# Batch 0's attention scores straight from strided q in two 64x64 tiles; w_in's first parts in four buffers; batch 1's first k and q behind batch 0's last v

## The chip, the cores and the metric

The kernel runs on one core of a Trainium2 chip. The metric is the time of one execution in device microseconds, the median of several runs. A NeuronCore has five engines that each work through their own instructions in order: TensorE (PE; its weight loads are shown as PEld), VectorE (DVE), ScalarE (ACT), GpSimd (POOL) and SyncE (SP), which here only issues DMA transfers. They wait for each other through semaphores.

## The reference, cut to what matters

Four batches (B = 4) of 576 tokens. A windowed attention over 8 heads of 64 feeds a second attention with 4 experts, of which two are chosen per token, and that feeds a mixing stage with sine and cosine and a last matrix product. Only the first two stages are touched.

```python
def _attn_ref(q, k, v):
    scores = scale * np.matmul(q, k.transpose(0, 1, 3, 2))
    rel = pos[:, None] - pos[None, :]
    mask = (rel >= 0) & (rel < 64)
    scores = np.where(mask, scores, -1000000000.0)
    attn = softmax(scores)
    return np.matmul(attn, v)

def _moe_ref(x, w_gate, wq, wk, wv, wo):
    logits = x @ w_gate
    for e in range(E):
        q, k, v = x @ wq[e], x @ wk[e], x @ wv[e]
        a = softmax(causal(scale * q @ k.T))
        out += chosen(e) * (a @ v @ wo[e])
```

(`softmax`, `causal` and `chosen` stand for the lines of the reference that spell them out.)

## The kernel before, in words

**The first attention** (`phase_a`, L236 to 316). The 8 heads are taken as 4 pairs (`hp`), one head in partitions 0 to 63 and one in 64 to 127. A pair's q lies as [128, 64, 9]: for each feature, 64 positions within a block by 9 blocks, so the 64 positions of one block stand 9 floats (36 bytes) apart. A pair is worked in three units (`g`) of three blocks of 64 queries; a batch has 12 units. I number batch 0's units 0 to 11. One unit is:

- q is copied into a tile `QD` [128, 3, 128] that is block diagonal: head 0's 64 columns in the upper half of the partitions, head 1's in the lower, zeros elsewhere, cleared once at the start (L167 to 170). In batch 0 DVE copies the upper half (L260) and ACT the lower (L258); in the later batches POOL copies both (`pool_mul`, L82, called from L256).
- three score products of 128x128 weights (`QD`) by 128 columns of k (L263), into a PSUM bank `as`;
- DVE adds the band mask and takes the row maximum (L268), ACT takes exponentials with row sums (L276), DVE sums and inverts (L281, L282), POOL multiplies (L283);
- PE transposes (L288, tile `apt`), DVE copies out (L291, `apv`; from batch 1 on ACT, L293), PE multiplies by v in 64-column tiles (L145 and L148, through `together`, tile `ao`), and the result is split into a high part (ACT, L87, `x0h`) and a low part (DVE, L90, `x0l`).

**The second attention** needs `w_in`, split into a high part `wih` (cast by ACT, L202) and a low part `wil` (POOL, L207; DVE for part of it, L209). `load_w` (L191) brings the four row blocks of its first 516 columns through two staging buffers (pool tag `bms`), then the rest. `vg_gates` (L346) makes values and gates from x (tile `vg`, 60 gate products a batch), `qk` (L319) makes queries and keys (tile `qk`), and `attn` (L403) does the attention; there POOL scales by the gates (L453, tiles `bms` and `bpd`).

**What sets the order.** The Python code yields after pieces of work, and `merge` (L45) interleaves several such generators by costs written by hand; the tile framework then schedules each engine's instructions from its own model of time. So a changed line can move instructions far behind it. The first `merge` (L651) runs batch 0's `phase_a` beside `load_w` for w_in's first columns; the second (L657) runs `qk(0, 0)`, `vg_gates(0)`, half of batch 1's `phase_a` and the rest of w_in. All loads of q, k, v and w_in after the first stand on SP's queue in one order. `fetch` (L219) loads a pair's q and k; `tc.issue_after(x)` keeps an instruction behind x in the schedule. v has four buffers, q and k two each.

## Time and profile before

| | |
|---|---|
| median of 3 runs | 528.53 us (528.49 to 529.69) |
| profiled execution | 528.16 us, of which span 526.4 us |
| busy: PE | 506.6 us (96%), 4372 instructions |
| busy: ACT | 329.6 us (63%) |
| busy: DVE | 323.1 us (61%) |
| busy: POOL | 304.6 us (58%) |
| read from HBM | 31.28 MB |

The profile is of one execution. Its span runs from the first to the last instruction. An fp32 product leaves two records on PE, so three products are shown as x6. A line number can be that of a helper: L93 to L95 are one three-part product, L145 and L148 the products issued through `together`, L82 is `pool_mul`.

### The profile page before, as it was taken

The numbers are of one execution on the slowest core, as the hardware profiler recorded it, in microseconds if no ns is written. First come the engines' busy times: TensorE is split into PE (matmuls) and PEld (weight loads), VectorE is DVE, ScalarE is ACT, GpSimd is POOL, SyncE is SP. The second block draws the span as 40 slices with busy tenths as digits, with TensorE's granted clock in tenths as the row PEclk, the third lists the DMA queues.
The fourth block names the chain that finished last, engine by engine and source line by source line (L and its number), as shares of the span: only waits on it lengthen the run. The fifth ranks groups of instructions, "written<-read, shape, count | busy, mean of one in ns | idle before, by whom it ended". The sixth has DMA issues, their size and how long they took to land.

```text
span 526.4 us, 12343 instructions
## 1 busy us (share of the span) xinstructions
PE 506.6 (96%) x4372; PEld 475.5 (90%) x4372; DVE 323.1 (61%) x1244; ACT 329.6 (63%) x1045; POOL 304.6 (58%) x464
## 2 busy tenths in 40 slices
PE   8879999999999999999998999999999999999997
PEld 6669888899998998989787998999999999999997
DVE  5876887858778597558988787553325324533312
ACT  7977698866878768677788977551437136523410
POOL 5798789664848842247876676951475226531420
PEclk9999999999999999999999999999999999999999
DMA  7865224222314421112004121002000200011002
GB/s 248 253 185 169 97 60 147 64 67 92 103 34 134 142 76 32 32 29 73 37 2 159 62 82 42 1 0 80 12 2 1 68 24 1 1 57 35 1 1 91
DMA packets 21086, 36.80 MB, mean 70 GB/s; under 512 B 2336, under 2 KB 13600, under 8 KB 21024
## 3 DMA queue, kind: packets, MB, share of 16 engines
q1 hardware_dynamic: 19008, 31.22, 18.7%
q10 hardware_dynamic: 2016, 4.79, 2.7%
q8 instruction: 35, 0.57, 0.5%
q14 instruction: 27, 0.22, 0.2%
HBM read 31.28 MB, written 4.72 MB: 68 GB/s over the span
## 4 chain that ended last, share of the span: by engine, by line
PE 70%; DVE 11%; ACT 6%; POOL 6%; issue 3%; DMA 3%; ACTq 0%; POOLq 0%; DVEq 0%
PE y L95 6%; PE y L93 6%; PE y L94 6%; PE as L263 3%; PE c L95 3%; PE c L94 3%; PE c L93 3%; PE th L93 3%; PE th L95 3%; PE th L94 3%; PE bpt L464 2%; PE qk L93 2%; PE qk L95 2%; PE qk L94 2%; PE apt L288 2%
## 5 line engine op out<-in xcount | busy, mean ns | idle before, releaser
L90 POOL TENSOR_TENSOR z<-zf,z 128x256 fp32r<-128x256 f32 x72 | 52.9, 749 | 87.3 <-ACT z L87 86.9
L93 PE MATMUL y<-wkh,z 128*128 128x288 f32 x288 | 86.4, 301 | 0.5 <-DVE x2T L595 0.5
L94 PE MATMUL y<-wkl,z 128*128 128x288 f32 x288 | 85.3, 296 | 0.0
L95 PE MATMUL y<-wkh,z 128*128 128x288 f32 x288 | 84.7, 297 | 0.0
L276 ACT ACTIVATE ams<-ams,anm 128x128 f32<-128x128 f32 x144 | 56.6, 396 | 4.5 <-DVE anm L268 4.1
L93 PEld LDWEIGHTS y<-wkh,z 128*128 128x128 f32 x288 | 54.2, 188 | 1.4 <-DVE x2T L595 0.6
L94 PEld LDWEIGHTS y<-wkl,z 128*128 128x128 f32 x288 | 54.2, 188 | 0.0
L95 PEld LDWEIGHTS y<-wkh,z 128*128 128x128 f32 x288 | 53.9, 188 | 0.0
L283 POOL TENSOR_TENSOR ams<-ams,arc 128x384 f32<-128x384 f32 x48 | 40.8, 850 | 18.5 <-DVE arc L282 7.7
L87 ACT CAST z<-zf 128x256 fp32r<-128x256 f32 x72 | 27.6, 404 | 37.6 <-DVE zf L562 15.7
L441 ACT ACTIVATE bms<-bms,bnm 64x64 f32<-64x64 f32 (+4 forms) x80 | 45.0, 563 | 8.5 <-DVE bnm L436 7.9
L82 POOL TENSOR_SCALAR QD<-qt 64x192 f32<-64x192 f32 x72 | 39.6, 551 | 16.0 <-PE as L263 10.1
L562 DVE TENSOR_TENSOR zf<-xk,ang 128x256 f32<-128x256 f32 x64 | 25.4, 420 | 36.4 <-ACT ang L549 19.4
L547 ACT ACTIVATE ang<-ang 128x256 f32<-128x256 f32 x36 | 14.6, 416 | 51.9 <-DVE ang L546 51.8
L263 PE MATMUL as<-kt,QD 128*128 128x128 f32 x288 | 43.5, 288 | 3.1 <-ACT x0h L87 1.3
L263 PEld LDWEIGHTS as<-kt,QD 128*128 128x128 f32 x288 | 37.5, 197 | 6.8 <-ACT x0h L87 1.5
L268 DVE CUSTOM_DVE_ANT_0 ams<-as,cst 128x128 f32<-128x128 f32 x144 | 34.7, 283 | 6.3 <-PE as L263 3.1
L93 PE MATMUL th<-wth,cx 128*128 128x256 f32 x128 | 36.5, 285 | 2.1 <-DVE bnm L436 1.5
L436 DVE CUSTOM_DVE_ANT_0 bms<-bs,mb 64x64 f32<-64x64 f32 (+4 forms) x80 | 32.5, 423 | 9.3 <-PE bs L434 4.9
L94 PE MATMUL th<-wtl,cx 128*128 128x256 f32 x128 | 36.0, 281 | 0.0
L608 DVE SCALAR_TENSOR_TENSOR x2T<-c,x2T 128x288 f32<-128x288 f32 x32 | 14.5, 457 | 34.2 <-PE c L95 34.0
L95 PE MATMUL th<-wth,cx 128*128 128x256 f32 x128 | 35.4, 283 | 0.0
(198 smaller groups left out, 1742.3 us busy)
## 6 DMA issues: line engine op xcount, KB each, us to landing
vt<-in_dram SPq DMA_DIRECT2D x48, 192.0 KB, 3.1
kt<-in_dram SPq DMA_DIRECT2D x15, 320.0 KB, 3.0
qt<-in_dram SPq DMA_DIRECT2D x16, 288.0 KB, 3.2
out_dram<-x2T SPq DMA_DIRECT2D x32, 144.0 KB, 1.8
w64k<-in_dram SPq DMA_DIRECT2D x5, 576.0 KB, 3.7
w64k<-in_dram ACTq DMA_DIRECT2D x4, 576.0 KB, 3.7
w64t<-in_dram SPq DMA_DIRECT2D x4, 512.0 KB, 3.8
w64c<-in_dram ACTq DMA_DIRECT2D x8, 256.0 KB, 2.8
```

Source lines behind the costliest of these rows:

```text
L82: nc.gpsimd.tensor_scalar(out=out, in0=in_, scalar1=by, scalar2=1.0, op0=ALU.mult, op1=ALU.mult)
L87: nc.scalar.copy(out=dst_h, in_=src)
L90: eng_l.tensor_sub(out=dst_l, in0=src, in1=f32(dst_h))
L93: nc.tensor.matmul(out, wh, xh, start=first, stop=False)
L94: nc.tensor.matmul(out, wh, xl, start=False, stop=False)
L95: nc.tensor.matmul(out, wl, xh, start=False, stop=last)
L263: nc.tensor.matmul(s[:, i, :], QD[g][:, i], kt[:, 64 * blk : 64 * blk + 128], start=True, stop=True)
L268: nc.vector.tensor_tensor_reduce(out=ms[:, i, :], in0=s[:, i, :], in1=ma0 if (g == 0 and i == 0) else ma1, scale=-0.125, scalar=3.0e38, op ...
L276: nc.scalar.activation(out=ms[:, i, :], in_=ms[:, i, :], func=AF.Exp, bias=nm[:, i : i + 1], scale=-1.0, accum_out=sm[:, i, 0:1],)
L283: nc.gpsimd.tensor_mul(out=ms, in0=ms, in1=rc.unsqueeze(2).to_broadcast([P, 3, P]))
L436: nc.vector.tensor_tensor_reduce(out=ms[:m, a:z], in0=s[:m, : z - a], in1=mb[:m, mo + a : mo + z], scale=-0.125, scalar=nm[:m, 0:1] if ci ...
L441: ex = nc.scalar.activation(out=ms[:m, :w], in_=ms[:m, :w], func=AF.Exp, bias=nm[:m, ci : ci + 1], scale=-1.0, accum_out=ss[:m, i, 0:1])
```

## The change

Four things are changed.

1. In batch 0 a unit's scores no longer go through `QD`. For each of the three blocks, two products of 64x64 weights are issued, one per head: the weights are q itself, read from its load tile at the stride of 9 floats, and the 64 rows of one head in k are the moving part. Head 0 uses partitions 0 to 63 of its operands and of the result, head 1 64 to 127. The six products go through `together`, so they stand behind each other in the schedule. The clearing of `QD` moves behind that of `KL`.
2. The four row blocks of w_in's first 516 columns are staged in four buffers, two of tag `bms` and two of tag `zc` (which w_o's staging uses later), instead of two.
3. `paced` replaces `delay`: the costs that `merge` counts for `load_w` are 0.75, 0.1, 0.1, 0.1, 0.35 instead of 0.9 and then 0.1 each, with the same total.
4. Batch 1's and later loads of k and q are scheduled behind the last load of v of batch 0.

```diff
--- before.py
+++ after.py
@@ -165,9 +165,6 @@
 
 
     QD = [ap.tile([P, 3, P], F32, name=f"QD{i}") for i in range(3)]
-    for i in range(3):
-        nc.vector.memset(QD[i][0:64, :, 64:128], 0.0)
-        nc.gpsimd.memset(QD[i][64:128, :, 0:64], 0.0)
 
     AS = [ap.tile([P, 3, 2], F32, name=f"AS{i}") for i in range(4)]
     BS = [bp.tile([P, 2, 2], F32, name=f"BS{i}") for i in range(4)]
@@ -187,12 +184,15 @@
     for e in range(E):
         z = slice(64 - 64 * (e % 2), 128 - 64 * (e % 2))
         nc.gpsimd.memset(f32(KL[e][z]), 0.0)
+    for i in range(3):
+        nc.vector.memset(QD[i][0:64, :, 64:128], 0.0)
+        nc.gpsimd.memset(QD[i][64:128, :, 0:64], 0.0)
 
     def load_w(src, n, dst_h, dst_l, tag):
-        pool, bufs = (bp, 2) if tag == "bms" else (cp, 2)
         for c in range(n):
             h, l = dst_h(c), dst_l(c)
-            st = pool.tile([P, h.shape[1]], F32, tag=tag, bufs=bufs, name=f"wst{c}")
+            pool, home = (cp, "zc") if tag == "zc" or tag == "both" and c >= 2 else (bp, "bms")
+            st = pool.tile([P, h.shape[1]], F32, tag=home, bufs=2, name=f"wst{c}")
             with tc.issue_after(last_load[0].ins):
                 nc.sync.dma_start(st, src[c * P : (c + 1) * P])
             w = h.shape[1]
@@ -210,6 +210,7 @@
             yield 0.1
 
     last_load = [None]
+    last_v = [None]
     late = [None]
     gated = [None]
     X = {b: xbuf[b % 2] for b in range(B)}
@@ -229,8 +230,9 @@
             nc.sync.dma_start(qt, qT[b, hp])
             last_load[0] = nc.sync.dma_start(kt, kT[b, hp])
         else:
-            last_load[0] = nc.sync.dma_start(kt, kT[b, hp])
-            nc.sync.dma_start(qt, qT[b, hp])
+            with tc.issue_after(last_v[0].ins):
+                last_load[0] = nc.sync.dma_start(kt, kT[b, hp])
+                nc.sync.dma_start(qt, qT[b, hp])
         return qt, kt
 
     def phase_a(b, hps):
@@ -243,25 +245,31 @@
             for g in range(3):
                 n = f"{b}{hp}{g}"
                 vt = ap.tile([P, 3, 2, D], F32, tag="vt", bufs=4, name=f"vt{n}")
-                nc.sync.dma_start(vt, vw[b, hp, :, 3 * g : 3 * g + 3])
+                v = nc.sync.dma_start(vt, vw[b, hp, :, 3 * g : 3 * g + 3])
+                if b == 0:
+                    last_v[0] = v
                 if b == 0 and hp == 0 and g == 2:
                     nc.sync.dma_start(cst[:, 3 * P :], consts[:, 3 * P :])
                 if b == 0 and 0 < hp < NP - 1 and g == 0:
                     ahead[0, hp + 1] = fetch(0, hp + 1)
                 s = bank([P, 3, P], "bs" if b == 0 and (g + hp) % 3 else "as", f"as{n}")
-                for h in range(2):
-                    r = slice(64 * h, 64 * h + 64)
-                    src = qt[r, :, 3 * g : 3 * g + 3].rearrange("p d n -> p n d")
-                    if b > 0:
-                        pool_mul(QD[g][r, :, r], src, 1.0)
-                    elif h:
-                        nc.scalar.copy(out=QD[g][r, :, r], in_=src)
-                    else:
-                        nc.vector.tensor_copy(out=QD[g][r, :, r], in_=src)
-                for i in range(3):
-                    blk = 3 * g + i
-                    nc.tensor.matmul(s[:, i, :], QD[g][:, i],
-                                     kt[:, 64 * blk : 64 * blk + 128], start=True, stop=True)
+                src = qt[:, :, 3 * g : 3 * g + 3].rearrange("p d n -> p n d")
+                if b == 0:
+
+                    for f in together():
+                        for i in range(3):
+                            blk = 3 * g + i
+                            for h in range(2):
+                                r = slice(64 * h, 64 * h + 64)
+                                f(s[r, i, :], qt[r, :, blk], kt[r, 64 * blk : 64 * blk + 128], start=True, stop=True)
+                else:
+                    for h in range(2):
+                        r = slice(64 * h, 64 * h + 64)
+                        pool_mul(QD[g][r, :, r], src[r], 1.0)
+                    for i in range(3):
+                        blk = 3 * g + i
+                        nc.tensor.matmul(s[:, i, :], QD[g][:, i],
+                                         kt[:, 64 * blk : 64 * blk + 128], start=True, stop=True)
                 ms = ap.tile([P, 3, P], F32, tag="ms", bufs=4, name=f"ams{n}")
                 nm = ap.tile([P, 3], F32, tag="nm", bufs=4, name=f"anm{n}")
                 for i in range(3):
@@ -644,12 +652,18 @@
         yield cost
         yield from gen
 
+    def paced(costs, gen):
+        yield costs[0]
+        for cost in costs[1:]:
+            next(gen)
+            yield cost
+
 
     warm = bank([P, KN['WM']], "g", "warm")
     for _ in range(WARM):
         nc.tensor.matmul(warm, mb[:, :P], mb[:, : KN['WM']], start=True, stop=True)
     merge((20, phase_a(0, (0, 1, 2, 3))),
-          (KN["CW"][4], delay(0.9, load_w(w_in[:, :W0], NC, lambda c: wih[:, c, :W0], lambda c: wil[:, c, :W0], "bms"))))
+          (KN["CW"][4], paced((0.75, 0.1, 0.1, 0.1, 0.35), load_w(w_in[:, :W0], NC, lambda c: wih[:, c, :W0], lambda c: wil[:, c, :W0], "both"))))
     pool_mul(mb[:, S - P :], cst[:, 3 * P : 4 * P], 1.0)
     for i in range(2):
         nc.gpsimd.memset(VD[i][0:64, :, 1], 0.0)
```

The new order on three engines, word for word; in the names, digits are batch, pair and unit (`ams011` is batch 0, pair 1, unit 1 of the pair) and what follows the underscore is a buffer's number. Line numbers of the change are by its own file, so L284 there is L276 of the kernel before, L271 is L263, L291 is L283 and L461 is L453.

ACT from its first computing instruction on, before:

```order
L258 ACT_TABLE_LOAD
L258 COPY QD0_95<-qt00_135 64x3x64
L258 COPY QD1_96<-qt00_135 64x3x64
L258 COPY QD2_97<-qt00_135 64x3x64
L258 COPY QD0_95<-qt01_141 64x3x64
L276 ACTIVATE ams000_153,AS1_105<-ams000_153,anm000_154 128x128 x3
L258 COPY QD1_96<-qt01_141 64x3x64
L276 ACTIVATE ams001_188,AS2_106<-ams001_188,anm001_189 128x128 x3
L258 COPY QD2_97<-qt01_141 64x3x64
L276 ACTIVATE ams002_224,AS3_107<-ams002_224,anm002_225 128x128 x2
L258 COPY QD0_95<-qt02_253 64x3x64
L276 ACTIVATE ams002_224,AS3_107<-ams002_224,anm002_225 128x128
```

and with the change:

```order
L284 ACT_TABLE_LOAD
L284 ACTIVATE ams000_154,AS1_99<-ams000_154,anm000_155 128x128 x3
L284 ACTIVATE ams001_190,AS2_100<-ams001_190,anm001_191 128x128 x3
L284 ACTIVATE ams002_227,AS3_101<-ams002_227,anm002_228 128x128 x3
L284 ACTIVATE ams010_267,AS0_98<-ams010_267,anm010_268 128x128 x3
L284 ACTIVATE ams011_303,AS1_99<-ams011_303,anm011_304 128x128 x3
L284 ACTIVATE ams012_339,AS2_100<-ams012_339,anm012_340 128x128 x3
L87 CAST x0h_88<-ao000_172 128x192
L202 CAST wih_73<-wst0_406 128x516
L202 CAST wih_73<-wst1_446 128x516
L284 ACTIVATE ams020_379,AS3_101<-ams020_379,anm020_380 128x128 x2
L202 CAST wih_73<-wst2_486 128x516
```

The copies of q are gone, the exponentials of the first six units follow each other, and the four casts of w_in (three of them shown) come behind them.

PE around `qk000`, the first q/k projection of batch 0 (`as110` is a score unit of batch 1), before:

```order
L93 MATMUL vg00_617<-wih_73,x0h_88 128x260
L94 MATMUL vg00_617<-wil_74,x0h_88 128x260
L263 MATMUL as110_850<-kt11_845,QD0_95 128x128 x3
L95 MATMUL vg00_617<-wih_73,x0l_89 128x260
L93 MATMUL vg02_776<-wih_73,x0h_88 128x260
L94 MATMUL vg02_776<-wil_74,x0h_88 128x260
L145 MATMUL ao032_581<-apv032_579,vt032_555 64x64
L148 MATMUL ao032_581<-apv032_579,vt032_555 64x64 x5
L93 MATMUL qk000_599<-x0h_88,wih_73 128x288
L94 MATMUL qk000_599<-x0l_89,wih_73 128x288
```

and with the change, from the same place on:

```order
L93 MATMUL vg00_629<-wih_73,x0h_88 128x260
L94 MATMUL vg00_629<-wil_74,x0h_88 128x260
L145 MATMUL ao032_593<-apv032_591,vt032_566 64x64
L148 MATMUL ao032_593<-apv032_591,vt032_566 64x64 x5
L95 MATMUL vg00_629<-wih_73,x0l_89 128x260
L93 MATMUL vg02_788<-wih_73,x0h_88 128x260
L94 MATMUL vg02_788<-wil_74,x0h_88 128x260
L93 MATMUL qk000_611<-x0h_88,wih_73 128x288
```

and, seven rows further on, from the ninth of that projection's twelve products on:

```order
L95 MATMUL qk000_611<-x0h_88,wil_74 128x288
L93 MATMUL qk000_611<-x0h_88,wih_73 128x288
L94 MATMUL qk000_611<-x0l_89,wih_73 128x288
L95 MATMUL qk000_611<-x0h_88,wil_74 128x288
L271 MATMUL as100_649<-kt10_644,QD0_95 128x128 x3
L95 MATMUL vg02_788<-wih_73,x0l_89 128x260
```

Before, `as100`, `as101`, `as102` and `as110` stand ahead of `qk000`; now the first of them, `as100`, follows that projection's twelve products. Ahead of `qk000` stand all 12 units of batch 0 and 32 gate products in both.

POOL in the second half of batch 0's first attention (`QD` from `qt10` is batch 1's q, `wil` from 128x516 the low part of w_in's first columns), before:

```order
L207 TENSOR_TENSOR wil_74<-wst0_469,wih_73 128x516
L283 TENSOR_TENSOR ams011_298<-ams011_298,arc011_306 128x384
L207 TENSOR_TENSOR wil_74<-wst1_473,wih_73 128x516
L283 TENSOR_TENSOR ams012_333<-ams012_333,arc012_341 128x384
L82 TENSOR_SCALAR QD0_95<-qt10_631 64x3x64 x2
L283 TENSOR_TENSOR ams020_372<-ams020_372,arc020_380 128x384
L82 TENSOR_SCALAR QD1_96<-qt10_631 64x3x64 x2
L207 TENSOR_TENSOR wil_74<-wst2_512,wih_73 128x516
L283 TENSOR_TENSOR ams021_407<-ams021_407,arc021_415 128x384
L82 TENSOR_SCALAR QD2_97<-qt10_631 64x3x64 x2
L283 TENSOR_TENSOR ams022_442<-ams022_442,arc022_450 128x384
L207 TENSOR_TENSOR wil_74<-wst3_551,wih_73 128x516
```

and with the change:

```order
L207 TENSOR_TENSOR wil_74<-wst0_406,wih_73 128x516
L207 TENSOR_TENSOR wil_74<-wst1_446,wih_73 128x516
L207 TENSOR_TENSOR wil_74<-wst2_486,wih_73 128x516
L291 TENSOR_TENSOR ams020_379<-ams020_379,arc020_387 128x384
L207 TENSOR_TENSOR wil_74<-wst3_526,wih_73 128x516
L291 TENSOR_TENSOR ams021_419<-ams021_419,arc021_427 128x384
L291 TENSOR_TENSOR ams022_459<-ams022_459,arc022_467 128x384
L291 TENSOR_TENSOR ams030_499<-ams030_499,arc030_507 128x384
L291 TENSOR_TENSOR ams031_539<-ams031_539,arc031_547 128x384
L291 TENSOR_TENSOR ams032_575<-ams032_575,arc032_583 128x384
L82 TENSOR_SCALAR QD0_95<-qt10_643 64x3x64 x2
L82 TENSOR_SCALAR QD1_96<-qt10_643 64x3x64 x2
```

The splits of w_in stand closer together, and the q tiles of batch 1 come only behind batch 0's last product (`ams032`).

On SP's queue the four loads of w_in's first columns now follow pair 3's q and k, ahead of v of unit 4; before, the third and fourth stood behind v of units 6 and 7, and batch 1's first q ahead of v of unit 4. Batch 1's first k and q now follow the last v of batch 0.

## Rows read from the trace of the kernel before

**Rows 1.** Windows; stretch, then busy us (records) of each engine, PEclk, DMA share, GB/s.

```profile
4.74:41.05 36.31, 30.43 (x308) 25.74 (x309) 27.49 (x164) 30.63 (x122) 27.31 (x43) 1.00 0.77 239
...
28.00:44.00 16.00, 13.34 (x142) 11.71 (x141) 12.02 (x62) 12.22 (x52) 15.20 (x23) 1.00 0.64 193
44.00:60.00 16.00, 16.00 (x159) 15.61 (x158) 11.33 (x63) 12.43 (x49) 10.49 (x22) 1.00 0.23 67
...
35.88:64.53 28.65, 28.38 (x283) 27.15 (x282) 21.24 (x106) 19.90 (x77) 22.29 (x45) 1.00 0.41 123
```

**Rows 2.** Chain of waits, in order of time: start us, us, what.

```profile
39.60 0.67 PE as L263 x6
40.27 0.12 PE vg L95
...
40.62 0.20 PE ao L145
...
41.12 0.33 PE qk L93
...
42.90 0.33 PE apt L288 x3
```

**Rows 3.** Waits of PE, 4.74 to 41.05: us in total, times, longest.

```profile
PE ao L145 <- DVE apv L291: 2.0, 4, 0.7
PE as L263 <- ACT x0h L87: 1.3, 1, 1.3
```

**Rows 4.** Groups of instructions, 4 to 45 us: shapes, count, busy us, mean ns.

```profile
L283 POOL TENSOR_TENSOR ams<-ams,arc 128x384 f32<-128x384 f32 x16 | 13.4, 841 | 3.8 <-DVE arc L282 2.4 <-ACT ams L276 1.1
...
L82 POOL TENSOR_SCALAR QD<-qt 64x192 f32<-64x192 f32 x15 | 8.3, 554 | 0.6
...
L291 DVE COPY apv<-apt 128x384 f32<-128x384 f32 x12 | 6.5, 542 | 0.3 <-PE apt L288 0.2
L258 ACT COPY QD<-qt 64x192 f32<-64x192 f32 x12 | 6.0, 532 | 2.3 <-DMA qt<-in_dram 1.2 <-PE as L263 0.9
...
L87 ACT CAST x0h<-ao 128x192 fp32r<-128x192 f32 x12 | 3.6, 297 | 0.0
L282 DVE RECIPROCAL arc<-arc 128x3 f32<-128x3 f32 x16 | 2.7, 169 | 0.3
...
L281 DVE TENSOR_REDUCE arc<-AS 128x3 f32<-128x6 f32 x16 | 2.5, 154 | 6.1 <-ACT ams L276 6.0
...
L207 POOL TENSOR_TENSOR wol<-wst,woh 128x384 fp32r<-128x384 f32 x2 | 2.0, 1008 | 0.1
```

**Rows 5.** Timeline of ACT: start us, us, engine, line, operation, count.

```profile
7.00 0.40 ACT L276 ACTIVATE ams<-ams,anm 128x128 f32<-128x128 f32 x1
...
21.80 0.40 ACT L276 ACTIVATE ams<-ams,anm 128x128 f32<-128x128 f32 x1
...
22.97 0.30 ACT L87 CAST x0h<-ao 128x192 fp32r<-128x192 f32 x1
23.16 0.62 ACT L202 CAST wih<-wst 128x516 fp32r<-128x516 f32 x1
23.69 0.40 ACT L276 ACTIVATE ams<-ams,anm 128x128 f32<-128x128 f32 x1
```

**Rows 6.** Timeline of PE, value products of the second attention in two column tiles.

```profile
299.94 0.32 PE L145 MATMUL o<-bpT,vg 128*64 128x128 f32 x1
299.94 0.32 PE L148 MATMUL o<-bpT,vg 128*64 128x128 f32 x1
300.10 0.27 PE L145 MATMUL o<-bpT,vg 128*64 128x128 f32 x1
300.11 0.93 PE L148 MATMUL o<-bpT,vg 128*64 128x128 f32 x13
300.96 0.42 PE L95 MATMUL x<-oh,wol 128*128 128x320 f32 x1
```

**Rows 7.** Timeline of POOL, the four scalings into bpd.

```profile
63.06 1.49 POOL L453 TENSOR_SCALAR bpd<-bms,bsm,gw 64x64 f32<-64x64 f32 x4
```

## The prediction

> **What bounds the kernel now.** I read the windows first, then the chain of waits, PE's waits, and the engines' timelines in the first 65 us. The windows show PE full from 44 to 60 us, and not full before: from 4.74 to 41.05 it is busy for 30.43 of 36.31 us, with ACT at 30.63, DVE at 27.49 and POOL at 27.31 [rows 1]. Even those 30.43 us are not full pace. At the pace that the chain shows, a unit's three score products take 0.67 us, its three transposes 0.33, its six value products 0.50 (40.62 to 41.12), one gate product 0.12 [rows 2]. By the program's order PE has issued 16 score units (12 of batch 0, 4 of batch 1), 12 units of transposes, 12 of value products and 32 gate products when `qk000`, the first q/k projection, starts at 41.12: 10.7 + 4.0 + 6.0 + 3.8 = 24.5 us of work in 36.4. So 11.9 us are lost there, and PE's waits name DVE and ACT [rows 3]. ACT is busy 84% of that stretch [rows 1] and sets the pace.
>
> **The change, part by part.**
>
> *Copies of q removed.* Batch 0 loses 12 copies on DVE and 12 on ACT, those on ACT at 532 ns [rows 4], 6.4 us. What ACT must still do until batch 0's attention ends is 36 exponentials, three in 1.17 us (21.80 to 22.97), 12 casts of x at 0.19, and four casts of w_in at 0.53 [rows 5]: 14.0 + 2.3 + 2.1 = 18.4 us. The first exponential starts at 7.00 [rows 5]; it follows the warm-up matmuls and the loads, which stay. At ACT's share of 84% the last one ends at 7.0 + 18.4/0.84 = 28.9. Behind it, for the last unit, come reduction and reciprocal (0.15 + 0.17), POOL's product 0.84, DVE's copy 0.54 [rows 4], transposes 0.33 and value products 0.50 [rows 2]: 2.5 us. Three gate products stand between that and `qk000` in the new order, 0.3 more, so it starts at **31.7** instead of 41.12.
>
> *Score products in two 64x64 tiles.* A unit is now six products, twelve records, instead of three and six. No row of this trace has two tiles that differ in rows, so I bound the price. The low end is today's 0.67. The nearest rows are the value products of the second attention: 64 columns of weights, 128 moving columns, two column tiles. Their records start in pairs within 0.01 us, and sixteen of them take from 299.94 to 300.96, 1.02 us [rows 6], or 0.128 a pair; six pairs are 0.77. The high end is that nothing runs side by side and the weights, now read at a stride of 36 bytes, load slower: the copies that read q at this stride took 532 ns on ACT, where a cast of as many elements a partition in sequence took 297 [rows 4], 1.79 times; twelve steps of 0.11 x 1.79 are 2.4 us. I take 0.8, by the two-tile rows as the nearest. PE's own sum until `qk000` is then 12 x (0.8 + 0.33 + 0.50) + 3.8 = 23.4 us from 4.74; with half of the 3.3 us of the two largest waits [rows 3] it ends at 29.8. ACT still ends last.
>
> The Trainium skill (SBUF — State Buffer, the section on Door 1) says that SBUF has lines of 16 bytes and that each access to a new line pays a penalty, which four-byte elements at 36 bytes always do. By that rule ACT's 532 against 297 is expected and the strided weights would pay too; the row of pairs, whose weights lie in sequence, says nothing of it. By the rule with the two tiles side by side a unit would cost 6 x 0.20 = 1.2 us, `qk000` would start at 34.6, and 3.8 us of the gain would be left.
>
> *What is not yet done at 31.7.* In the order before, four score units of batch 1 stand ahead of `qk000`; in the new order none do. PE owes 4 x 0.67 = 2.7 us then. The gain at equal work is 41.12 - 31.7 - 2.7 = **6.7 us**.
>
> *POOL, moved work.* Before, POOL builds batch 1's q tiles between batch 0's products, and it is busy 15.20 of 16 us from 28 to 44 [rows 1]. Now they follow batch 0's last product. Take the last scaling of the second attention's first two tiles (`bpd001`), the last of the four that start at 63.06 and end at 64.55 [rows 7]. From the end of batch 0's last product, 35.88, to 64.53 POOL was busy 22.29 us [rows 1]. In the new order the same piece holds two pairs of q tiles more (4 x 0.55), one split of w_o more (1.01), one of w_in, a sixth as wide (an estimate of 0.3 from that row), and two products of 0.84 fewer [rows 4]: 24.1 us. Its start is 28.9 + 0.3 + 0.84 = 30.0. At POOL's share of that stretch before, 22.29 of 28.65 or 78%, it ends at 60.9, 3.6 us earlier; at the 95% of 28 to 44 it ends at 55.4, 9.1 earlier. So POOL allows between 3.6 and 9.1, and PE 6.7. I take **5.2**, midway between 3.6 and 6.7.
>
> *w_in's parts and the loads.* On SP's queue four parts of 258 KB now stand together ahead of unit 4's v, where two parts and batch 1's first q (288 KB) stood: 228 KB more, 1.0 us at the 239 GB/s of that stretch [rows 1]. I cost it at nothing: a unit's v is used last in it, behind five units of exponentials. If that cover is gone, the queue waits once, 1 us. The third and fourth part no longer wait for POOL to empty a buffer. Batch 1's first k and q come after the last v and are needed by POOL at 30.0; if they are later, POOL waits with all its products behind it.
>
> *Edits with one answer.* The clearing of the q tiles moves by a few instructions at the start, where POOL and DVE have nothing due, and batch 0 leaves those tiles alone.
>
> After that the work is the same, and another order can give or take about 1.5 us, which I only estimate. The profiled execution took 528.16 us and the runs' median is 528.53; 528.5 - 5.2 = **523.3 us**.
>
> **The rivals.**
>
> 1. *The tiles run one after the other.* Twelve records of 0.11 and 0.15 for the change of tiles (the first pair of the two-tile rows starts 0.16 before the second): 1.47 us a unit. PE then needs 12 x (1.47 + 0.33 + 0.50) + 3.8 = 31.4 us from 4.74, and with half the waits `qk000` starts at 37.8. The gain is 41.12 - 37.8 - 2.7 = 0.6: **527.9**, no change. Against it stand the pairs of the rows with two column tiles; for it, that those share all their rows, and that no row here has two row tiles. The Trainium skill (TensorEngine Tiling (Array Packing), Gotcha 1: PSUM Pressure) says that different row tiles cannot access the same PSUM bank at once. Here both tiles of a unit write one bank, so by that rule this rival would hold; since they write different partitions of it, I give it a small chance only.
>
> 2. *Strided weights make PE the bound (slower).* The same sum, with the price of a unit left open, is level with today at 1.52 us a unit, and each 0.1 above costs 1.2 us. At the high end, 2.4, it gives 528.5 + 10.6 = **539.1**. It decides as soon as both hold, slow loads and no overlap. ACT's copies speak for the first, the pairs against the second.
>
> 3. *POOL's work comes too late (slower).* It is level when POOL does its 24.1 us between 30.0 and 64.53, a share of 70%. In 44 to 60 us its share was 10.49 of 16, 66% [rows 1]; at that share it ends 2.0 us later than today: **530.5**. Against it: there is always a q tile to be built next, as in 28 to 44, where the share was 95%.
>
> 4. *The copies were hidden, or the order gives the gain back later.* If ACT's freed time only becomes waiting, `qk000` moves but PE stalls behind it: between 0 and 1.5 us are left, **527.5**. ACT's 84% and PE's waits on ACT and DVE speak against it.
>
> **How the numbers follow.** The forecast gets 0.66, rival 1 0.14, rival 2 0.05, rival 3 0.09, rival 4 0.06. The forecast's own range is 519.7 (ACT at 93%, a gain of 8.8, which POOL at 95% allows) to 526 (POOL at 75%). Rivals 1 and 4 lie at 527 to 528.5, and a little over if rival 1's waits are more: 519.7 to 529.3 leaves out rivals 2 and 3 and a small tail below. A difference of 0.3%, 1.6 us, is about what a measurement of this kernel tells from no change. Faster by more than that: the forecast and a part of rivals 1 and 4, 0.69; the same: 0.17; slower: 0.14.
>
> **What would show it.** In the profile of the changed kernel the twelve records of a score unit should stand in pairs that start together, 0.8 us a unit; `qk000` should start near 31.7; POOL should be busy for over 80% from 30 to 59 us; the four scalings should end near 59; and PE should have no idle time of note between 32 and 59. The forecast is wrong if a score unit takes over 1.4 us, if POOL waits for batch 1's first q, or if PE's idle time after 60 us grows by more than 3 us.

## The result, and the profile after

The changed kernel took 534.93 us (median of 5 runs, 531.75 to 537.04) against 528.53 for the kernel before: a ratio of 1.0106, 95% interval [1.0069, 1.0144]. It is slower by 1.1%, clear of the noise; the forecast was 523.3, with a range up to 529.3. The profiled execution took 533.75 us, span 532.0.

The windows of the changed kernel, in the columns of [rows 1], the first four over the same stretches, then four of 5 us:

```profile
4.74:41.05 36.31, 31.26 (x363) 25.87 (x364) 20.89 (x121) 21.03 (x90) 19.08 (x29) 0.91 0.62 200
28.00:44.00 16.00, 15.68 (x166) 13.27 (x163) 9.81 (x43) 7.75 (x32) 7.21 (x13) 0.90 0.67 216
44.00:60.00 16.00, 15.05 (x137) 14.26 (x136) 12.12 (x67) 14.18 (x57) 14.43 (x26) 1.00 0.37 107
35.88:64.53 28.65, 27.70 (x258) 26.21 (x257) 20.52 (x102) 19.57 (x74) 23.22 (x44) 1.00 0.53 165
20.00:25.00 5.00, 2.06 (x27) 1.58 (x27) 2.77 (x17) 3.45 (x14) 4.77 (x6) 0.92 0.39 127
25.00:30.00 5.00, 4.83 (x43) 3.63 (x43) 3.09 (x21) 2.94 (x15) 1.65 (x2) 0.50 0.18 46
265.00:270.00 5.00, 2.41 (x16) 1.48 (x14) 4.90 (x15) 4.60 (x13) 5.00 (x6) 1.00 0.00 0
270.00:275.00 5.00, 4.96 (x31) 4.57 (x30) 2.48 (x11) 2.98 (x8) 4.77 (x5) 0.66 0.01 3
```

ScalarE lost its copies, and did not use the room: 21.03 busy us where it had 30.63 [rows 1], in the same time. TensorE's granted clock, 1.00 in [rows 1], is 0.91 over the first stage: half, the 1.2 GHz level, from 25 to 30 us, and 0.66 on average from 270 to 275, each time behind a stretch with a hole in it (2.06 and 2.41 busy us of 5). The profile gives a mean granted clock of 0.990 over 532.0 us, so 5.3 us of full pace are missing; the kernel before had 1.000.

TensorE's timeline of the changed kernel, the first stage (start, us, line, operation, count, idle before and what ended it):

```profile
11.54 0.38 PE L145 MATMUL as<-kt,qt 64*64 64x128 f32 x1
11.55 0.38 PE L148 MATMUL as<-kt,qt 64*64 64x128 f32 x1
11.76 0.28 PE L145 MATMUL as<-kt,qt 64*64 64x128 f32 x1
11.77 0.76 PE L148 MATMUL as<-kt,qt 64*64 64x128 f32 x9
12.47 0.55 PE L296 MATMUL apt<-cst,ams 128*128 128x128 f32 x3
...
13.87 0.27 PE L145 MATMUL ao<-apv,vt 128*64 128x64 f32 x1
...
15.76 0.27 PE L145 MATMUL ao<-apv,vt 128*64 128x64 f32 x1
...
17.67 0.27 PE L145 MATMUL ao<-apv,vt 128*64 128x64 f32 x1
...
22.48 0.24 PE L145 MATMUL ao<-apv,vt 128*64 128x64 f32 x1 [2.84 <-issue]
...
40.17 0.30 PE L93 MATMUL qk<-x0h,wih 128*128 128x288 f32 x1
```

The tiles do what was forecast: the two of a pair start 0.01 us apart, and a unit takes 0.93 us (11.54 to 12.47). But `qk000` starts at 40.17, against 41.12 before and 31.7 forecast. The one long hole is in front of the fourth group of value products, unit 3's. The groups 4 to 45 us of the changed kernel, in the columns of [rows 4], show that the strided weight loads are the slower ones, 211 ns against 159 for as many columns of v in sequence, and that the exponentials waited 10.5 us in all; before, ScalarE waited between 7 and 32 us for nothing but w_in's loads, 1.7 us. The 159 takes in records at half clock; the last two rows are the same groups from 5 to 22 us, all at full clock, and give 211 against 137 (v's loads fill all 128 partitions, q's 64, so the two differ in more than the stride):

```profile
L284 ACT ACTIVATE ams<-ams,anm 128x128 f32<-128x128 f32 x37 | 14.5, 393 | 10.5 <-DVE anm L276 8.5 <-DVE x0l L90 1.1 <-DVE arc L290 0.8
...
L148 PEld LDWEIGHTS as<-kt,qt 64*64 64x64 f32 x120 | 10.7, 211 | 0.0
...
L148 PEld LDWEIGHTS ao<-apv,vt 128*64 128x64 f32 x120 | 6.0, 159 | 0.0
...
L148 PEld LDWEIGHTS as<-kt,qt 64*64 64x64 f32 x98 | 8.5, 211 | 0.0
...
L148 PEld LDWEIGHTS ao<-apv,vt 128*64 128x64 f32 x30 | 1.3, 137 | 0.0
```

How the hole comes about is in ScalarE's and then VectorE's timeline:

```profile
15.98 0.30 ACT L87 CAST x0h<-ao 128x192 fp32r<-128x192 f32 x1
18.30 1.28 ACT L202 CAST wih<-wst 128x516 fp32r<-128x516 f32 x2 [2.02 <-DMA wst<-in_dram]
19.48 0.40 ACT L284 ACTIVATE ams<-ams,anm 128x128 f32<-128x128 f32 x1
19.87 0.39 ACT L284 ACTIVATE ams<-ams,anm 128x128 f32<-128x128 f32 x1
20.26 0.61 ACT L202 CAST wih<-wst 128x516 fp32r<-128x516 f32 x1
20.77 0.40 ACT L284 ACTIVATE ams<-ams,anm 128x128 f32<-128x128 f32 x1
```

```profile
21.29 0.16 DVE L289 TENSOR_REDUCE arc<-AS 128x3 f32<-128x6 f32 x1 [3.48 <-ACT ams L284]
21.49 0.17 DVE L290 RECIPROCAL arc<-arc 128x3 f32<-128x3 f32 x1
21.58 0.53 DVE L299 COPY apv<-apt 128x384 f32<-128x384 f32 x1
```

Three queues in a row, each in order: ScalarE's first cast of w_in waits 2.02 us for its load, and unit 6's exponentials stand behind it; VectorE's `arc` of unit 6 waits 3.48 us for the third of these; `apv` of unit 3, whose input is there since 18.7, stands behind that `arc`; TensorE's product of unit 3 needs `apv`. (The view names no releaser for that product. `apv` ends at 22.11 and it starts 0.37 us later; for unit 2 that gap is 0.48.)

The second hole is far from the change. TensorE, then VectorE, near 269 us; `ol` is the low part of the second attention's output, and the 448-column `bms` are its widest masked scores:

```profile
269.86 0.39 PE L478 MATMUL bdt<-cst,bpd 128*128 128x128 f32 x1 [1.88 <-DVE ol L90]
```

```profile
262.66 0.62 DVE L444 CUSTOM_DVE_ANT_0 bms<-bs,mb 128x448 f32<-128x448 f32 x1
...
268.48 0.44 DVE L444 CUSTOM_DVE_ANT_0 bms<-bs,mb 128x288 f32<-128x288 f32 x1
...
269.60 0.20 DVE L90 TENSOR_TENSOR ol<-o,oh 128x64 fp32r<-128x64 f32 x1
```

In the kernel before, VectorE has the 64-column `ol` ahead of those scores, and TensorE's windows there have neither the hole nor the fall of the clock:

```profile
259.93 0.22 DVE L90 TENSOR_TENSOR ol<-o,oh 128x64 fp32r<-128x64 f32 x1
260.26 0.62 DVE L436 CUSTOM_DVE_ANT_0 bms<-bs,mb 128x448 f32<-128x448 f32 x1
```

```profile
265.00:270.00 5.00, 4.62 (x41) 4.01 (x39) 4.03 (x16) 4.62 (x14) 4.82 (x8) 1.00 0.00 0
270.00:275.00 5.00, 5.00 (x48) 4.75 (x46) 4.58 (x21) 4.17 (x15) 3.04 (x6) 1.00 0.02 7
```

In these 10 us the changed kernel does 2.41 + 4.96 x 0.66 = 5.7 us of work at full pace, the kernel before 9.6. Of the 3.9 us between them 2.2 are idle time and 1.7 the half clock.

**Where the time went.** For each profiled run I took windows of 2.5 us over the whole span, multiplied TensorE's busy time by its granted clock, and summed from a time to the end: TensorE's work still to do. The table (span in the last column) says how much later (+) or earlier than in the kernel before the same work is left, in us, at six times of the kernel before.

| kernel | 40 | 60 | 230 | 255 | 275 | 310 | end |
|---|---|---|---|---|---|---|---|
| changed | +0.9 | +1.8 | +2.2 | +2.8 | +6.4 | +7.2 | +5.6 |
| w_in undone | +2.7 | +3.5 | +4.2 | +4.7 | +6.8 | +7.6 | +6.0 |
| w_in alone | +1.0 | +1.0 | +1.4 | +1.9 | +5.3 | +6.0 | +4.4 |
| k and q alone | -4.1 | -2.2 | -2.1 | -2.0 | -1.4 | -1.5 | -3.2 |
| tiles alone | +4.8 | +4.8 | +5.1 | +5.7 | +10.5 | +12.9 | +11.2 |
| tiles undone | -2.9 | -0.9 | -0.6 | -0.6 | 0.0 | -0.1 | -1.7 |
| late order | +1.1 | +2.3 | +2.4 | +2.1 | +1.7 | +6.7 | +5.1 |
| casts behind | -1.4 | -0.6 | -0.6 | -0.1 | +4.6 | +7.1 | +5.5 |
| mended | -5.8 | -3.9 | -4.5 | -4.5 | -3.8 | -4.2 | -5.8 |
| mended, casts later | -4.5 | -3.0 | -0.6 | -0.1 | +4.9 | +7.3 | +5.6 |

The changed kernel loses twice: 1.8 us in the first 60, and 3.6 between 255 and 275, where no line of the program was changed. The other rows are the experiments below. Each row is one execution; the medians beside the experiments are of several. By about 60 us the change was to have gained 5.2 us and had lost 1.8, so 7.0 us of the miss lie there; 3.8 lie behind.

### The profile page after: what moved, and what is told of

Same layout as the page of the kernel before. It is cut to its first block, busy times and chain, and to the rows that moved or that the text cites. A ratio compares the mean times of both kernels' runs of the same rounds, so it can differ in the third digit from the quotient of the medians.

```text
span 532.0 us, 12457 instructions
## 1 busy us (share of the span) xinstructions
PE 510.0 (96%) x4444; PEld 479.3 (90%) x4444; DVE 319.5 (60%) x1232; ACT 323.0 (61%) x1033; POOL 305.1 (57%) x464
## 4 chain that ended last, share of the span: by engine, by line
PE 74%; DVE 8%; ACT 7%; POOL 4%; DMA 3%; issue 3%; SPq 0%; DVEq 0%; POOLq 0%; ACTq 0%
PE y L93 7%; PE y L95 7%; PE y L94 7%; ACT ams L284 3%; PE c L95 3%; PE c L94 3%; PE c L93 3%; PE th L93 3%; PE th L94 3%; PE th L95 3%; PE as L271 3%; PE apt L296 2%; PE bpt L472 2%; PE bs L440 2%; PE ao L148 2%
## 5 line engine op out<-in xcount | busy, mean ns | idle before, releaser
L93 PE MATMUL y<-wkh,z 128*128 128x288 f32 x288 | 85.8, 300 | 0.0
L95 PE MATMUL y<-wkh,z 128*128 128x288 f32 x288 | 83.6, 297 | 0.0
L284 ACT ACTIVATE ams<-ams,anm 128x128 f32<-128x128 f32 x144 | 56.6, 397 | 18.0 <-DVE anm L276 15.8
L291 POOL TENSOR_TENSOR ams<-ams,arc 128x384 f32<-128x384 f32 x48 | 39.6, 828 | 26.0 <-DVE arc L290 15.1
L444 DVE CUSTOM_DVE_ANT_0 bms<-bs,mb 64x64 f32<-64x64 f32 (+4 forms) x80 | 32.6, 422 | 11.4 <-PE bs L442 8.7
L276 DVE CUSTOM_DVE_ANT_0 ams<-as,cst 128x128 f32<-128x128 f32 x144 | 34.6, 284 | 7.9 <-PE as L148 4.8
L90 POOL TENSOR_TENSOR cu<-x2T,cu 128x288 fp32r<-128x288 f32 x32 | 25.5, 821 | 18.1 <-ACT cu L87 18.1
L552 DVE TENSOR_SCALAR ang<-th 128x256 f32<-128x256 f32 x36 | 15.2, 421 | 31.7 <-PE th L95 31.4
```

Source lines behind the costliest of these rows:

```text
L90: eng_l.tensor_sub(out=dst_l, in0=src, in1=f32(dst_h))
L93: nc.tensor.matmul(out, wh, xh, start=first, stop=False)
L95: nc.tensor.matmul(out, wl, xh, start=False, stop=last)
L276: nc.vector.tensor_tensor_reduce(out=ms[:, i, :], in0=s[:, i, :], in1=ma0 if (g == 0 and i == 0) else ma1, scale=-0.125, scalar=3.0e38, op ...
L284: nc.scalar.activation(out=ms[:, i, :], in_=ms[:, i, :], func=AF.Exp, bias=nm[:, i : i + 1], scale=-1.0, accum_out=sm[:, i, 0:1],)
L291: nc.gpsimd.tensor_mul(out=ms, in0=ms, in1=rc.unsqueeze(2).to_broadcast([P, 3, P]))
```

## The experiments

All were timed in 5 rounds beside the kernel before, whose median there was 528.97 to 529.55; each gives its median and its ratio to the kernel before, with the 95% interval. The numbers of units are the front part's.

**The parts, one by one.** The first theory (A) was that four w_in loads stand ahead of v on SP's queue, and that TensorE's clock falls behind the wait for v. *w_in undone* and *tiles, w_in and k/q alone* test it.

```diff
-          (KN["CW"][4], paced((0.75, 0.1, 0.1, 0.1, 0.35), load_w(w_in[:, :W0], ..., "both"))))
+          (KN["CW"][4], delay(0.9, load_w(w_in[:, :W0], ..., "bms"))))
```

> The changed kernel with one part undone: w_in's first parts again in two buffers and spread over the queue; the tiles and batch 1's k and q behind batch 0's v stay. Theory A (the four w_in loads stand ahead of unit 4's v on SP's queue, TensorE idles 2.84 us for that v and its granted clock then falls to 0.50 for a stretch): v of unit 4 is issued before 16 us, no idle time of TensorE over 1.5 us between 15 and 30 us, granted clock over 0.97 in 20 to 35 us, first q/k projection 4 us or more earlier than the 40.17 of the changed kernel, time 525 to 529 us. Rival B (the score tiles or the strided weights cost): the time stays at 532 to 536 us, and TensorE's scores are what it waits for. Rival C (batch 1's k and q come too late behind the last v): first q/k projection is early, but POOL idles for batch 1's first q and the time stays at 531 to 535 us. Rival D (the later order of the program, with the second fall of the clock near 270 us): time over 531 us with a quiet first 40 us.

Measured: 535.28 us, 1.0131 [1.0112, 1.0150]. Nothing is gained, so A falls in this form: TensorE has two holes, 2.21 us until 21.42 and 2.69 until 27.34, and ScalarE's casts waited 5.3 us for w_in's loads between 12 and 32 us. *w_in alone* is the kernel before with the other side of that diff (the four buffers and the pacing):

> The kernel before with w_in's first parts in four buffers and their loads early, and nothing else of the change. Theory A: the loads of w_in stand ahead of some v here too, though one of the four goes behind unit 4's; TensorE idles 1 to 3 us for a v near 20 us and the time is 530 to 534 us; if the three loads ahead are not enough for that, it is 528 to 530 us. Rivals B and C: within 0.3% of the kernel before, 527 to 530 us. Rival D: 530 us or more without an idle stretch near 20 us.

532.99 us, 1.0081 [1.0058, 1.0104]: slower, by the table 1.9 us of it until 255 us and 3.4 more from there to 275. *k and q alone* is the kernel before with

```diff
+            with tc.issue_after(last_v[0].ins):
                 last_load[0] = nc.sync.dma_start(kt, kT[b, hp])
                 nc.sync.dma_start(qt, qT[b, hp])
```

> The kernel before with batch 1's first k and q loaded behind the last v of batch 0, and nothing else of the change. Theory A: the v loads move up, none of batch 1's score units stands ahead of the first q/k projection, which comes 1 to 3 us earlier than 41.12; the work is only moved, 527 to 530 us. Rival C: POOL waits for batch 1's first q behind the last v, 531 to 534 us. Rivals B and D: 527 to 530 us.

525.04 us, 0.9932 [0.9916, 0.9947]. This part is a gain by itself; `qk000` starts at 35.6. POOL waited up to 4.2 us for batch 1's first q, so that wait (rival C) is not what costs. *Tiles alone* is the kernel before with the diff's score loop, the moved clearing of the q tiles and no copies:

> The kernel before with batch 0's scores in two 64x64 tiles from q at a stride and no copies of q, and nothing else of the change. Theory A: the copies are gone from ScalarE and VectorE, a pair of tiles runs side by side as in the changed kernel (about 0.93 us a unit), v of unit 4 is issued before 16 us, the first q/k projection starts at 34 to 38 us, time 524 to 528 us. Rival B: 531 us or more, TensorE being what the exponentials wait for. Rivals C and D: 525 to 529 us.

538.67 us, 1.0181 [1.0158, 1.0204], the slowest of all, so that B (the tiles cost) looked right. Its waits from 12 to 32 us (who waited for whom: us in total, times, longest) look like the changed kernel's:

```profile
DVE arc L288 <- ACT ams L283: 9.2, 6, 3.7
ACT wih L202 <- DMA wst<-in_dram: 5.7, 3, 2.1
```

**v ahead, a filler, tiles undone.** In the changed kernel each w_in load was put behind the last v issued by then:

```diff
-            with tc.issue_after(last_load[0].ins):
+            with tc.issue_after(last_v[0].ins):
                 nc.sync.dma_start(st, src[c * P : (c + 1) * P])
```

> The changed kernel with one line more: each w_in load is ordered behind the last v issued by then, so units 4, 5 and 6 have their v ahead of the first w_in load on SP, and the other three w_in loads stand between later v. Theory A (a v behind w_in on SP's queue leaves TensorE idle in one stretch, and its granted clock falls after it): v of unit 4 issued by 14.5 us instead of 17.54, no idle of TensorE over 1.5 us before 30 us, granted clock above 0.97 in 20 to 35 us, first q/k projection at 32 to 37 us instead of 40.17, time 524 to 530 us. Rival B (tiles or strided weights cost as such, whatever the queue): 533 us or more. Rival D (the later order of the program has its own fall of the clock near 270 us): the first 40 us are quiet, yet the time is 529 to 533 us with the granted clock under 0.9 near 270 us.

535.09 us, 1.0110 [1.0087, 1.0133]. The clock stayed at 1.00 from 15 to 40 us (one hole of 1.60 us), `qk000` started at 37.5, and nothing was left of it at 60 us: TensorE waited 2.43 us for POOL's q tile of batch 1 until 47.62, with a granted clock of 0.77 from 45 to 50 us. With the loads later still the time was 535.45, 1.0123 [1.0106, 1.0141]. Theory A falls; I had also misread the hole as unit 4's, while it is unit 3's, whose v was issued at 5.12.

> The changed kernel with the score products of unit 9 issued five times instead of once (24 products more, the same operands and the same bank; about 2.8 us by the 0.70 us that six pairs take), right ahead of unit 4's product, where TensorE idled 2.84 us for v. SP's queue stays as in the changed kernel. Theory A, its part on the clock: TensorE has no idle stretch there, granted clock stays at 1.00 in 20 to 35 us, and though work is added the time falls by 2 to 5 us, to 530 to 533 us. If the granted clock doesn't matter or falls for another reason: time unchanged or longer, 534 to 538 us. Rival B: 536 us or more, as more tile products run. Rival D: 532 to 535 us with the fall near 270 us as before.

```diff
-                        for i in range(3):
+                        for i in [*range(3)] * (5 if hp == 3 and g == 0 else 1):
```

535.12 us, 1.0123 [1.0094, 1.0151], inconclusive: the products ran from 24.15 to 29.5 us, behind the hole and not in it, since unit 3's products stand ahead of them. The filler therefore tells nothing about what the clock's falls cost apart from the holes. With the tiles undone (copies and whole products again, the rest of the change kept):

> The changed kernel with the tiles undone: copies of q and whole products again, w_in in four buffers and batch 1's k and q behind batch 0's v kept. Theory A: three w_in loads stand ahead of unit 4's v on SP here too, TensorE idles for it if its exponentials are far enough, which they are less than with the tiles: 526 to 532 us, with the clock's fall deciding. Rival B (the tiles cost as such): 525 to 528 us, well under the changed kernel. Adding the three parts measured alone (w_in +4.0, k and q -3.9) gives 529 us.

526.05 us, 0.9944 [0.9930, 0.9957]. So without the tiles w_in in four buffers costs little (526.05 against 525.04 for k and q alone), and with both other parts the tiles cost 8.9 us. On TensorE they add 12 x (0.93 - 0.67) = 3.1 us of work at most. Of the 7.3 us between the two profiled spans, 2.7 are there at 60 us and the rest comes later. Two orders differ: VectorE takes `anm` of unit k+1 ahead of `arc` of unit k in the kernel before and in this one, behind it in most units with the tiles; and near 260 us.

**VectorE's order (theory E).** The changed kernel, with `arc` of a unit behind `anm` of the next:

```diff
+                    with tc.issue_after(nxt.ins):
                         nc.vector.tensor_reduce(out=rc, in_=sm, op=ALU.add, axis=AX.X)
```

> The changed kernel with only VectorE's order in batch 0 changed: the sums of a unit's exponentials (arc) are queued behind the masked scores (ams, anm) of the next unit; everything else of the change stays, SP's queue too. Theory E (with the tiles VectorE's queue holds arc of unit k ahead of anm of unit k+1, so ScalarE's exponentials of k+1 wait for those of k to travel over arc, x0l, apv and anm; it waited 1.15 to 1.21 us a unit in the kernel with v ahead): these waits of ScalarE for anm fall under 0.3 us a unit in the units before 17 us, first q/k projection 1.5 to 4 us earlier than 40.17, time 529 to 533 us, the four w_in loads ahead of unit 4's v keep their stretch near 20 us. Rival B (the tile products cost as such on TensorE): 533 us or more, first q/k projection unchanged within 1 us. Rival A (SP's queue alone): unchanged, 534 to 536 us.

532.46 us, 1.0068 [1.0044, 1.0093]; `qk000` at 37.7. The time is as E had it, its sign is not: between 10 and 32 us ScalarE's waits for `anm` were 4.5 us, and 3.2 in the changed kernel. With v ahead and two units between:

> The kernel with v ahead (535.09 us), and VectorE's order in batch 0 changed: arc of unit k behind anm of unit k+2. Theory E: ScalarE is no longer idle for anm between 12 and 27 us (under 1 us in all), its busy share there above 85 per cent instead of 68, the first q/k projection at 31 to 35 us instead of 37.5, TensorE's granted clock 1.00 there; the scores of batch 1 then still wait for POOL near 45 us, so that part may be given back: 524 to 531 us. Rival B: 533 us or more, and the first q/k projection not under 36.5 us. Rival D (the later order): first q/k projection early, time still 531 to 534 us with a fall of the clock near 270 us.

533.98 us, 1.0087 [1.0070, 1.0104]. At 30 us it was 3.6 us ahead of the kernel before by equal work; then TensorE waited 1.63 and 0.97 us for the parts of w_in, and its clock was 0.70 and 0.62 from 25 to 35. The gain was real, and the next late thing took it.

**The order near 260 us (theory D).** The changed kernel, with batch 3's shifts of the token weights (`wtuk`) queued behind the late `ol`:

```diff
+            done = split(oh[:, q0 : q0 + m], ol[:, q0 : q0 + m], o[:, :m], nc.scalar, nc.vector)
+            if (b, ep, t) == (3, 0, 0):
+                gated[0] = done
```

> The changed kernel with nothing of batch 0 touched; only, in batch 3, VectorE's shifts of the converted token weights (wtuk) are queued behind the first low part of the outputs (ol, 128x64) instead of ahead of it, so that every engine's order is the changed kernel's up to about 255 us. Theory D (the other half of the loss is the later order: at equal TensorE work left, the changed kernel falls back from +2.8 at 255 us to +6.1 at 280 us, TensorE idle 1.88 us for ol and its granted clock 0.66 behind that): the idle stretch and the fall near 270 us are gone, time 1.5 to 4 us less than 534.9, 531 to 533.5 us. Rivals A, B and E (all in the first 60 us): no difference, 534 to 536 us.

533.13 us, 1.0069 [1.0043, 1.0094]. Windows of this run:

```profile
265.00:270.00 5.00, 4.70 (x40) 4.32 (x40) 4.18 (x11) 4.37 (x12) 4.83 (x6) 1.00 0.30 103
...
285.00:290.00 5.00, 4.46 (x21) 4.46 (x21) 4.24 (x16) 4.55 (x9) 3.08 (x4) 0.50 0.02 5
```

The loss near 270 is gone (+1.7 at 275), and the same work, put off, makes a new hole at 284 with half the clock behind it; at 310 us the table has +6.7 against the changed kernel's +7.2. So this order moves the loss and doesn't mend it. A mend with E, v ahead, earlier w_in loads and this one took 534.07, 1.0091 [1.0069, 1.0112]: ScalarE's casts waited 2.4 us for their loads again.

**The casts (theory F).** Only the three-queue chain read above: the changed kernel with ScalarE's casts queued behind the last exponentials written.

```diff
+                with tc.issue_after(last_exp[0].ins):
                     nc.scalar.copy(out=h[:, cut:], in_=st[:, cut:])
```

> The changed kernel with only this: each of ScalarE's four casts of w_in (wih) is queued behind the last exponential of the units written by then, so behind units 6 to 9 instead of between the exponentials of units 5 and 6. SP's queue, the tiles and VectorE's rule stay. Theory F (TensorE's idle 2.84 us near 20 us comes over three queues: ScalarE's first cast waits 2.02 us for w_in's load with unit 6's exponentials behind it; VectorE's arc of unit 6 waits 3.48 us for these; apv of unit 3 stands behind that arc, and TensorE's product of unit 3 behind apv): the idle stretch near 20 us falls under 1.2 us, granted clock 1.00 in 20 to 35 us, first q/k projection 2 to 5 us earlier than 40.17, time 530.5 to 533 us (the loss near 270 us stays, so not under 529). If v or the tiles decide instead: 534 to 536 us.

531.97 us, 1.0051 [1.0027, 1.0074]. Windows:

```profile
20.00:25.00 5.00, 3.43 (x50) 2.79 (x52) 3.07 (x20) 3.98 (x16) 3.82 (x5) 1.00 0.19 55
25.00:30.00 5.00, 3.33 (x46) 2.56 (x42) 3.42 (x22) 3.45 (x15) 3.84 (x5) 1.00 0.36 101
...
265.00:270.00 5.00, 3.26 (x13) 2.82 (x14) 3.79 (x15) 3.99 (x11) 4.82 (x7) 0.60 0.01 3
```

No hole over 1.20 us and no fall of the clock in the first stage, -0.6 instead of +1.8 at 60 us: F holds for that loss in the trace; the medians are less clear, since the interval of the ratio touches the changed kernel's. The late loss is there as before.

**All of it.** The tiles, four buffers, k and q behind v; three of w_in's loads behind v of unit 6 and one behind unit 7's, the casts behind the exponentials of unit 8 and later, `anm` of k+2 ahead of `arc` of k (each by the lines above). What is new is that the loads are written first and the casts later. No line holds the order near 260 us here: these pacing numbers are ones with which the planned order there is that of the kernel before:

```diff
-    paced((0.75, 0.1, 0.1, 0.1, 0.35), load_w(...))
+    paced((0.5, 0.02, 0.02, 0.02, 0.4, 0.1, 0.1, 0.1, 0.14), load_w(...))
```

> The tiles, w_in in four buffers and batch 1's k and q behind batch 0's v, with w_in's loads issued together behind the v of units 4 to 6, their casts on ScalarE queued behind the exponentials of units 8 to 10, anm of unit k+2 ahead of arc of unit k on VectorE, and a later order near 260 us that is that of the kernel before (ol of 64 columns ahead of the second conversion of token weights). Theories E, F and D together: ScalarE over 85 per cent busy from 10 to 27 us, first q/k projection at 32 to 35.5 us, granted clock 1.00 before 40 us and near 270 us, 521 to 527 us, so faster than the kernel before and level with or ahead of batch 1's k and q behind v alone (525.0). Rival B (the tile products cost as such): 530 us or more. If POOL is what bounds 30 to 60 us once the projections start early, the gain of the first 35 us is given back there: 525 to 529 us.

523.25 us, **0.9885 [0.9861, 0.9909]**: faster than both kernels. Windows, TensorE's start of `qk000`, and two of VectorE's rows:

```profile
20.00:25.00 5.00, 4.21 (x61) 3.31 (x60) 4.66 (x27) 4.60 (x21) 4.46 (x5) 1.00 0.86 261
25.00:30.00 5.00, 4.89 (x60) 3.78 (x59) 3.15 (x16) 3.15 (x12) 4.78 (x6) 1.00 0.62 175
265.00:270.00 5.00, 4.36 (x42) 3.68 (x41) 4.94 (x18) 3.18 (x13) 4.19 (x8) 1.00 0.00 2
270.00:275.00 5.00, 5.00 (x41) 4.03 (x40) 3.98 (x19) 3.41 (x13) 2.61 (x5) 1.00 0.10 16
```

```profile
33.70 0.38 PE L93 MATMUL qk<-x0h,wih 128*128 128x288 f32 x1
```

```profile
250.70 0.22 DVE L90 TENSOR_TENSOR ol<-o,oh 128x64 fp32r<-128x64 f32 x1
...
255.60 0.62 DVE L471 CUSTOM_DVE_ANT_0 bms<-bs,mb 128x448 f32<-128x448 f32 x1
```

The 64-column `ol` is ahead of the widest masked scores here, as in the kernel before; in the changed kernel it is 7 us behind the first of them. Its twin differs in two numbers, the fifth and the last of that list (0.5 and 0.04 for 0.4 and 0.14):

> The kernel with everything mended (523.25 us), only the casts of w_in paced a unit later (behind the exponentials of units 9 to 11), by which the planned order near 260 us is again that of the changed kernel (ol of 64 columns behind the masked scores of the widest step). Theory D (that order costs by itself): the first 60 us within 1.5 us of the mended kernel, then 3 to 5 us lost between 255 and 300 us with the granted clock under 0.85 in one of the stretches there, 526 to 529 us. If the late order does not matter by itself: 522.5 to 525 us.

533.65 us, 1.0085 [1.0058, 1.0111]. Windows, and the same two rows of VectorE:

```profile
265.00:270.00 5.00, 3.12 (x16) 2.63 (x13) 3.98 (x14) 4.03 (x11) 4.80 (x7) 0.64 0.00 0
270.00:275.00 5.00, 5.00 (x33) 4.56 (x32) 2.87 (x11) 1.81 (x6) 4.74 (x6) 0.68 0.02 5
```

```profile
260.23 0.62 DVE L471 CUSTOM_DVE_ANT_0 bms<-bs,mb 128x448 f32<-128x448 f32 x1
...
267.16 0.20 DVE L90 TENSOR_TENSOR ol<-o,oh 128x64 fp32r<-128x64 f32 x1
```

At 60 us the two are 0.9 apart, at the end 11.4 (532.0 against 520.6): 3.0 more by 230 us, 0.5 by 255, 4.3 by 275, 2.8 by 310. So 7.1 us come between 255 and 310 us, where D puts the loss, more than the 3 to 5 expected; D doesn't explain the 3.0 us between 60 and 230, and their cause stays open.

The table bears D out. In the three others that have `ol` ahead of the widest scores (k and q alone, tiles undone, mended) 0.6 to 0.7 us go between 255 and 275 us; in the six that have it about 7 us behind (changed, w_in undone, w_in alone, tiles alone, casts behind, and this twin) 2.1 to 5.0; the late order run, which has it 1.7 us behind, loses 5.0 between 275 and 310. The first three and the kernel before are the four fastest of all. So much of what the parts seemed to cost one by one, the tiles above all, is which of the two orders the planner came to.

Last, the mended kernel with copies in place of tiles:

> The kernel with everything mended (523.25 us), with the tiles undone: copies of q on ScalarE and VectorE and whole products from them; w_in's loads, the casts behind the exponentials, VectorE's rule and batch 1's k and q stay. If the tiles are worth what the copies took on ScalarE (some 0.5 us a unit, 12 units): first q/k projection 2 to 5 us later than 33.7, 525 to 528 us. Rival B (tiles cost as such, and the mends alone made the gain): 520 to 523 us. If ScalarE's gain is given back on POOL: 523 to 525 us.

535.47 us, 1.0132 [1.0103, 1.0161]. `qk000` came at 41.3, TensorE waited 3.18 us for ScalarE's `x0h` until 37.81, and the order near 260 us was a third one. It tells that these mends suit the tiles, not what the tiles are worth by themselves: that stays open.

## Why the prediction was wrong, point by point

- *Copies removed: right as a quantity, wrong as a time.* The step that failed is "At ACT's share of 84% the last one ends at 7.0 + 18.4/0.84 = 28.9". ScalarE's share was 58% (21.03 of 36.31), and its last exponential of batch 0 started at 33.76. The 84% was the share of an engine that had copies to do while it waited; with them gone, the exponentials waited 10.5 us for VectorE and a cast 2.02 us for w_in's load. I counted ScalarE's work and left out who feeds it.
- *w_in's parts: "I cost it at nothing".* I looked only at v on SP's queue. The cover I named was that v is used late; the loads have another reader, the casts, and the order shown ahead of the prediction has them in front of unit 6's exponentials. Measured: 2.02 us on ScalarE, 3.48 on VectorE, 2.84 on TensorE, and half the clock behind it. Casts behind exponentials: 2.4 us back at 60 us.
- *"Another order can give or take about 1.5 us, which I only estimate".* This term is mis-sized, and against the kernel before it is the larger loss: +3.6 us here from 255 to 275 us, and 7.1 from 255 to 310 between two kernels that differ in two pacing numbers (10.4 in their medians, with a part that has another place). I compared orders around the change only.
- *The tiles: right in kind, a little dearer.* 0.93 us a unit against 0.8 taken, with the pair 0.01 us apart; rivals 1 (1.47) and 2 (1.52 and more) are refuted. The Trainium skill's rule against two row tiles in one PSUM bank (TensorEngine Tiling (Array Packing), Gotcha 1) is not borne out for tiles that write different partitions of it. The strided loads are the slower ones (211 against 137 ns at full clock). By the Trainium skill's rule on lines of 16 bytes (SBUF — State Buffer, Door 1) the prediction estimated 1.2 us a unit; the measured time lies between the 0.8 taken and that 1.2.
- *POOL: wrong as a term, though rival 3 didn't decide.* The four scalings were to end 3.6 to 9.1 us earlier and start 1.2 later, at 64.30 [rows 7 has 63.06]; POOL was busy 20.71 of the 29 us from 30 to 59, 71% and not over 80%. The sign that the prediction names, POOL waiting for batch 1's first q, came: that load is issued at 33.98, behind the last v, and POOL idles 2.62 us for it until 38.26. From 40 to 60 us the table loses 0.9 us in all, so this was not the main loss. With v ahead, where TensorE is earlier, its wait for POOL's q tile took the gain back: 2.43 us until 47.62.
- *Rivals.* Rival 4 (the freed time only becomes waiting, or the order gives the gain back) came nearest by its mechanism, and I priced it at 527.5 with 0.06; none of them had an in-order queue on ScalarE. With the queues mended `qk000` starts at 33.7 and the time is 523.25, close to the 31.7 and 523.3 of the forecast, but that is another kernel, and its late order helps it too.
- *What is not settled.* The mended kernel's gain was not split among its mends; each alone (532.46, 533.13, 531.97) has an interval that touches or overlaps the changed kernel's, so there the traces carry the argument. Why the planned order near 260 us flips was not tried, nor was that order held still while a part was changed in the first stage.

## What to carry to other kernels

Taking work off the busiest engine helps only as far as its queue has the next thing ready: before counting its work, read what stands at the head of each in-order queue, and which load or engine that waits for. Where a planner orders the program, compare the orders to the end and not only around the change; two orders that differ 230 us later cost more here (7.1 us) than the change was forecast to gain (5.2). And an engine that has lost its other work idles through each wait.

## What the runs showed that I had not expected

TensorE's granted clock fell to half behind a long hole: behind 2.84 us at 22.48 and 1.88 at 269.86 in the changed kernel, 1.74 at 267.07 with the casts behind. It did not fall behind 3.18 us at 37.81 in the mended kernel with copies, nor behind 1.67 at 287.29 with k and q alone, so the length of the hole alone does not tell. The kernels whose first trace shows a mean clock of 1.000 (before, k and q alone, tiles undone, mended) are the four fastest of all.
